# Sums of forms and of weights in place of the blocks they are made of, two places ahead of their splits; a first stage with two pieces fewer; the second weights loaded later

## The chip, the core and the metric

The kernel runs on one core of one Trainium2 chip. The metric is the device time of one execution in microseconds; a figure for a kernel is the median of several runs.

The core's engines work side by side, each through its own queue in order: TensorE (PE, with its weight loads shown apart as PEld), VectorE (DVE), ScalarE (ACT), GpSimd (POOL) and SyncE (SP). Here POOL and SP only issue transfers (DMA): SP loads, POOL stores.

## The reference

```python
def reference(A_x, A_dft_seq_re, A_dft_seq_im, A_dft_hid_re, A_dft_hid_im, B_x, B_w1, B_w3, B_w2, gate_w):
    x = A_x                                              # (1, 2048, 512)
    g = _sigmoid((x * gate_w).sum(-1, keepdims=True))
    a = x @ A_dft_hid_re.T                               # 512 -> 512, real part
    b = x @ A_dft_hid_im.T                               # imaginary part
    fnet = A_dft_seq_re @ a - A_dft_seq_im @ b           # 2048 x 2048 times 2048 x 512, twice
    gate, up = x @ B_w1, x @ B_w3                        # 512 -> 1376
    glu = (_silu(gate) * up) @ B_w2                      # 1376 -> 512
    return g * fnet + (1 - g) * glu
```

(The einsums are written here as products; all in fp32.)

## The kernel before

**Products in three matmuls.** Every fp32 operand is split in two tiles: `hi`, rounded by a copy on ACT (line 71), and `lo`, what is left, by a subtraction on DVE (line 74). A product is then hi·hi + hi·lo + lo·hi: three matmuls (line 81, `mm3`).

**Seven products in place of eight.** Each large product is cut into 2 x 2 blocks and done by a Strassen-Winograd scheme: seven products P1 to P7 of sums of blocks. Sums of the moving operand are called F1 to F4; those of the stationary one ("forms") are, for blocks a11, a12, a21, a22:

- P1: a11, P2: a12, P4: a22 (the blocks themselves)
- P5: a22 - a21
- P6: a11 subtracted from minus P5's sum, -(a22 - a21) - a11
- P7: a11 - a21
- P3: -a12 minus P6's sum

Sums with two minus signs go through `minus_sum` (line 77), one DVE instruction.

**Stages.** (1) The first stage, from the start to some 82 us: 14 steps of `sums_of` / `taken` / `forms_of` for x times the hidden DFT matrices; results go to DRAM as `ab`. (2) The items, to some 289 us: the 1376 columns of w1 and w3 in 11 chunks, `item(c)` for each; the gated products go to DRAM as `hsp`. In odd items and ahead of the first, `second` does an additional product in six parts: PE accumulates into `Yi`, ACT and DVE add what is there to `s` (lines 386 to 398), and PE goes on in the same bank when they have read it. (3) The blocks, to the end: `step` for w2 (m = 0) and for the two sequence DFT matrices (m = 1, 2), whose stationary forms were made in stages 1 and 2.

**Weights of a chunk.** `load_w(c)` loads `ws` (four blocks of 256 columns) on SP's queue, two items ahead. `prep_wa(c)` splits the first two blocks (three for the last chunk) into `wa`. `prep_wb(c)` first calls `sum_wb(c)`, which makes four sums in a fresh tile `wu` (lines 265 to 268), and then splits `wu` into `wb`. `prod` uses them by their place: 0 for F1, 1 for F2, 2 for F3, 3 for B22.

**Pieces of forms.** `forms(m, q, ks, keep)` returns a list of functions, one for the load of two tiles `r` (SP's queue) and one for each product in `ks`: split it into a tile `f` and store that to `fsp` on POOL's queue (with `keep`, the split stays in SBUF for the blocks). `ahead` puts the sum of the next product behind the split of the one before; the sum of the first product stands with the load. Sums P5, P6, P3 and P7 are written to halves of fresh tiles `m`. `inner_forms` does the same for a further product, with tiles `rl`, `ml`, `fl`. The list `later` holds 65 such pieces in order: three sets for m = 0, w2's last rows, three for m = 2, two for m = 1, the inner set. `work(2)` takes two of them at each of the steps 7 to 12 of the first stage (12 in all), and in each item the hooks h0 to h3 take one and h4 takes two. What needs other times is in `tasks`: a table from a step of the first stage to loads and preparations.

**Buffers and order.** Loaded blocks, sums, form tiles, results and some splits share one pool `f4` of 19 buffers (`raw` takes one). A tile takes the buffer of an older tile, and its first writer waits until the older tile's last users are done, a store from it among them. A planner puts the instructions of each engine in order before the kernel runs, by the order of the program and by its own estimate of when each could start; what goes through `pinned`, `keep_in_program_order` or `fetch` keeps the order of the program.

Of the kernel before, what the change touches and what calls it, by code (L numbers as in the profile page):

```python
# [28 lines left out]
def fnet_swiglu_gate_kernel(  # L29
# [17 lines left out]
    nc = tc.nc  # L47
# [11 lines left out]
    def raw(name, n=1024):  # L59
        return f4.tile([P, n], F32, tag="f4", name=name)  # L60

    def half(ap, n=2):
        return ap.rearrange("p (a n) -> p a n", a=n)
# [12 lines left out]
    def minus_sum(o, a, b):  # L76
        nc.vector.scalar_tensor_tensor(o, a, -1.0, b, op0=ALU.mult, op1=ALU.subtract)  # L77
# [181 lines left out]
        WA[c] = half(h, n // 256), half(l, n // 256)  # L259

    def sum_wb(c):
        w = half(WS[c], 4)
        u = raw(f"wu{c}")
        v = half(u, 4)
        nc.vector.tensor_sub(v[:, 0], w[:, 1], w[:, 3])
        minus_sum(v[:, 1], v[:, 0], w[:, 0])
        nc.vector.tensor_sub(v[:, 2], w[:, 0], w[:, 3])
        minus_sum(v[:, 3], v[:, 1], w[:, 2])
        WB[c] = u

    def prep_wb(c):
        if c not in WB:
# [64 lines left out]
    def prod(ps, w, k, xk, start, chain=True):  # L337
        for g in range(G):
            xh, xl = XF[g, xk]
            for q in range(2):  # L340
                sl = slice(q * P, (q + 1) * P)
                mm3(ps[:, g], w[0][:, k, sl], w[1][:, k, sl], xh[:, q], xl[:, q],
                    start and q == 0, q == 1, chain)
# [73 lines left out]
    def item(c, hooks):  # L417
        x, wa, wb = X[c], WA[c], WB[c]

        def part(n):  # L420
            if c % 2 and c + 2 < NC:
                second((c + 1) // 2, n)

        z = pair(3, f"Z{c}")
        u2, u4, g1 = raw(f"u2_{c}"), raw(f"u4_{c}"), None
        prod(x, wb, 1, "F2", False)
        pinned(nc.scalar.activation(u2, flat(x), AF.Copy))
        prod(z, wb, 2, "F3", True)
        pinned(nc.scalar.activation(u4, flat(z), AF.Copy))
        part(0)  # L430
        hooks[0]()
        if c + 1 < NC:
            first1(c + 1)
        if c + 2 == NC:
            begun(c + 1)
        part(1)
        hooks[1]()
        prod(x, wb, 0, "F1", False)
        nc.vector.tensor_add(u4, u4, flat(x))  # L439
        hooks[2]()  # L440
        part(2)
        prod(z, wa, 1, "F4", False)
        nc.vector.tensor_add(u2, u2, flat(z))
        nc.vector.tensor_mul(u2, u2, S1[c])
        store_h(c, 0, u2)
        part(3)
        hooks[3]()
        if c + 2 == NC:
            first2(c + 1)
        hooks[4]()  # L450
        prod(x, wb, 3, "B22", False)
        if c == NC - 1:
            put_score(1, flat(x), -1.0)
        g1 = raw(f"g1_{c}")
        nc.scalar.activation(g1, flat(x), AF.Silu, scale=-1.0)
        if c == NC - 1:
            nc.vector.tensor_mul(u4, u4, g1)
        else:
            nc.vector.scalar_tensor_tensor(u4, u4, -1.0, g1, op0=ALU.mult, op1=ALU.mult)
        store_h(c, 1, u4)  # L460
        part(4)
        part(5)
# [11 lines left out]
    NQS = {0: (NP + 1) // 2, 1: NQ, 2: NQ}  # L474
    A = {}

    def forms(m, q, ks, keep):

        n = width(m, q)
        st = {}  # L480

        def load():
            for h, src in enumerate(rows_of(m, q)):
                st[h] = raw(f"r{m}{q}{h}")
                nc.sync.dma_start(st[h][:, : 2 * n], src[:, : 2 * n])
            st["a11"], st["a21"] = (st[0][:, v * n : (v + 1) * n] for v in range(2))
            st["a12"], st["a22"] = (st[1][:, v * n : (v + 1) * n] for v in range(2))

        def total(k):
            if k in ("P5", "P3") or k == "P7" and "m" not in st:  # L490
                st["m"] = raw(f"m{m}{q}{k}")
            if k == "P5":
                src = st["m"][:, :n]
                nc.vector.tensor_sub(src, st["a22"], st["a21"])
                st["s5"] = src
            elif k == "P6":
                src = st["m"][:, n : 2 * n]
                minus_sum(src, st["s5"], st["a11"])
                st["s6"] = src
            elif k == "P3":  # L500
                src = st["m"][:, :n]
                minus_sum(src, st["a12"], st["s6"])
            elif k == "P7":
                src = st["m"][:, n : 2 * n]
                nc.vector.tensor_sub(src, st["a11"], st["a21"])
            else:
                src = st[{"P1": "a11", "P2": "a12", "P4": "a22"}[k]]
            st[k] = src

        def parts(k):  # L510
            src = st[k]
            pool, tag = (op, "op") if keep else (f4, "f4")
            t = pool.tile([P, 2, n], F32R, tag=tag, name=f"f{m}{k}{q}")
            split(t[:, 0], t[:, 1], src)
            if keep:
                A[m, k, q] = t
            else:
                nc.gpsimd.dma_start(fsp[m, PRODS.index(k), q, :, : 2 * n], flat(t.bitcast(F32)))  # L518

        return ahead(load, total, parts, ks)  # L520

    def ahead(load, total, parts, ks):

        def one(i):
            if i < 0:
                load()
            else:
                parts(ks[i])
            if i + 1 < len(ks):
                total(ks[i + 1])  # L530

        return [lambda i=i: one(i) for i in range(-1, len(ks))]

    def inner_forms():

        st = {}

        def cols(t, v):
            return t.rearrange("p (c h e) -> p c h e", c=4, h=2)[:, :, v]

        def quads(ap):
            return ap.rearrange("p (c e) -> p c e", c=4)

        def load():
            for h in range(2):
                st[h] = raw(f"rl{h}")
                for q in range(2):
                    nc.sync.dma_start(
                        st[h][:, q * 512 : (q + 1) * 512], ab[1, 1, 2 * h + q, :, 0].rearrange("p i e -> p (i e)"))

        def total(k):
            a11, a21, a12, a22 = cols(st[0], 0), cols(st[0], 1), cols(st[1], 0), cols(st[1], 1)
            if k in ("P5", "P3"):
                st["m"] = raw(f"ml{k}")
            lo, hi = quads(st["m"][:, :512]) if "m" in st else None, quads(st["m"][:, 512:]) if "m" in st else None
            if k == "P5":
                src = st["s5"] = lo
                nc.vector.tensor_sub(src, a22, a21)
            elif k == "P6":
                src = st["s6"] = hi  # L560
                minus_sum(src, st["s5"], a11)
            elif k == "P3":
                src = lo
                minus_sum(src, a12, st["s6"])
            elif k == "P7":
                src = hi
                nc.vector.tensor_sub(src, a11, a21)
            else:
                src = {"P1": a11, "P2": a12, "P4": a22}[k]
            st[k] = src  # L570

        def parts(k):
            src = st[k]
            t = f4.tile([P, 2, 512], F32R, tag="f4", name=f"fl{k}")
            split(quads(t[:, 0]), quads(t[:, 1]), src)
            nc.gpsimd.dma_start(lsp[PRODS.index(k)], flat(t.bitcast(F32)))

        return ahead(load, total, parts, ("P1", "P5", "P6", "P3", "P7", "P2", "P4"))

    def load_inner(k):  # L580
        t = A["L", k] = op.tile([P, 2, 4, P], F32R, tag="op", name=f"al{k}")
# [21 lines left out]
    todo = list(INNER)  # L603
# [349 lines left out]
    forms_of(2)  # L953
    later = []
    for q in range(NQS[0]):
        later += forms(0, q, PRODS, False)
    early = len(later)
    later += prep_w2l()
    for q in range(3):
        later += forms(2, q, [k for k in PRODS if k != "P2"], False)  # L960
    for q in range(2):
        later += forms(1, q, ("P1", "P5", "P6", "P3"), False)
    later += inner_forms()
# [1 line left out]
    def work(count):  # L965
        for _ in range(count):
            if later:
# [1 line left out]

    tasks = {2: lambda: load_x(1, "B11"), 3: lambda: load_x(1, "B12"),  # L970
             5: lambda: load_x(1, "B22"), 6: lambda: load_x(1, "B21"),
             7: lambda: load_w(0), 8: lambda: (load_bt(1), load_bt(0), load_w(1)), 9: lambda: (load_wp(0), sum_wb(0), sum_bt()),
             10: lambda: (prep_wa(0), prep_wb(0), sum_wp(0)), 11: lambda: (prep_bt("T3"), prep_bt("T4")),
             12: lambda: (prep_wp(0), prep_bt("T1"))}
    sums_of(0, (0,), True)
    sums_of(1, (0,), True)
    for n in range(len(DSEQ)):
        sums_of(n, (1,) if n < 2 else (0, 1))
        taken(n)
        forms_of(n + 3)  # L980
        tasks.get(n, lambda: None)()
        if 7 <= n < 13:
            work(2)
    first1(0)
    for n in (0, 3, 1, 4, 2, 5):
# [76 lines left out]
    todo += [lambda k=k, q=q: load_a(1, k, q) for k, _ in CHAIN[:4] for q in range(2)]  # L1062
    for i, f in enumerate(todo):
        TASKS.setdefault(AT[0, "P6", 0] + 2 * i if i < 4 else AT[1, "P1", 0] + 2 * i - 6, []).append(f)
    todo = forms(2, 3, [k for k in PRODS if k != "P2"], True)
    todo[:2] = [lambda fs=todo[:2]: [f() for f in fs]]
    todo += [lambda k=k, q=q: load_a(2, k, q) for k in LORDER for q in range(3)]
    for i, f in enumerate(todo):
# [74 lines left out]
```

## Time and profile before

| | us |
|---|---|
| median of 3 runs (701.94 to 702.03) | 701.95 |
| the profiled execution's own time | 703.77 |
| its span in the trace | 701.7 |

Busy shares, in tenths, in 40 slices of the span (17.5 us each):

```profile
PE   9999999999999999999999999999999999999997
PEld 7888888888888788888888888888888888888886
DVE  6999767697878976769998897679785976999985
ACT  6746356365555454474463474445534444544530
PEclk9999999999999999999999999999999999999999
DMA  8387955677887889678459969830989978898923
```

A digit 9 is 90% or more; PEclk is the granted TensorE clock, DMA the mean busy share of the core's 16 DMA engines. In lines of a timeline the columns are start, duration (us), engine, line, operation, `out<-in`, shape, and in brackets the engine's idle time ahead of it and what ended that. A form like `B<-cc` names tiles or DRAM tensors without their numbers.

### The profile page before, as it was taken

The numbers are of one execution on the slowest core, as the hardware profiler recorded it, in microseconds if no ns is written. First come the engines' busy times: TensorE is split into PE (matmuls) and PEld (weight loads), VectorE is DVE, ScalarE is ACT, GpSimd is POOL, SyncE is SP. The second block draws the span as 40 slices with busy tenths as digits, with TensorE's granted clock in tenths as the row PEclk, the third lists the DMA queues.
The fourth block names the chain that finished last, engine by engine and source line by source line (L and its number), as shares of the span: only waits on it lengthen the run. The fifth ranks groups of instructions, "written<-read, shape, count | busy, mean of one in ns | idle before, by whom it ended". The sixth has DMA issues, their size and how long they took to land.

```text
span 701.7 us, 8585 instructions
## 1 busy us (share of the span) xinstructions
PE 695.5 (99%) x3061; PEld 574.1 (82%) x3061; DVE 575.8 (82%) x646; ACT 356.3 (51%) x417; POOL 85.5 (12%) x136
## 2 busy tenths in 40 slices
PE   9999999999999999999999999999999999999997
PEld 7888888888888788888888888888888888888886
DVE  6999767697878976769998897679785976999985
ACT  6746356365555454474463474445534444544530
POOL 0012302131222220000000001000000020110110
PEclk9999999999999999999999999999999999999999
DMA  8387955677887889678459969830989978898923
GB/s 301 138 289 293 344 196 207 226 259 295 293 291 273 303 278 373 233 273 327 161 219 376 356 213 228 286 122 31 339 294 373 341 131 290 210 353 237 218 34 88
DMA packets 54602, 177.00 MB, mean 252 GB/s; under 512 B 5852, under 2 KB 6620, under 8 KB 54560
## 3 DMA queue, kind: packets, MB, share of 16 engines
q1 hardware_dynamic: 35312, 109.98, 44.9%
q0 software_dynamic: 19104, 66.34, 29.2%
q8 instruction: 24, 0.39, 0.2%
q14 instruction: 18, 0.15, 0.1%
q10 hardware_dynamic: 144, 0.13, 0.1%
HBM read 117.96 MB, written 58.47 MB: 251 GB/s over the span
## 4 chain that ended last, share of the span: by engine, by line
PE 91%; issue 5%; POOL 1%; DVE 1%; DMA 1%; DVEq 0%; POOLq 0%
PE P L81 55%; PE X L81 12%; PE dP L81 10%; PE Z L81 6%; PE Lx L81 3%; PE Yi L81 2%; DMA fsp<-f1P 1%; PE Y L81 1%; PE dP L205 1%; POOL fsp L518 1%; PE last L81 1%; PE wps L936 1%; POOL hsp L415 0%; DVE wu L77 0%; DVE s L353 0%
## 5 line engine op out<-in xcount | busy, mean ns | idle before, releaser
L71 ACT ACTIVATE zh<-B 128x1024 fp32r<-128x1024 f32 (+1 forms) x142 | 145.9, 1031 | 169.7 <-PE P L81 136.9
L74 DVE TENSOR_TENSOR zl<-B,zh 128x1024 fp32r<-128x1024 f32 (+1 forms) x142 | 167.1, 1183 | 45.9 <-ACT zh L71 39.0
L81 PE MATMUL P<-zh,f1P 128*128 128x512 f32 x320 | 99.9, 389 | 0.0
L81 PE MATMUL P<-zh,a2P 128*128 128x512 f32 x280 | 88.9, 389 | 0.0
L81 PE MATMUL P<-zh,a0P 128*128 128x512 f32 x280 | 87.6, 389 | 0.0
L677 DVE TENSOR_TENSOR B<-B,B 128x1024 f32<-128x1024 f32 (+1 forms) x70 | 83.6, 1204 | 1.2 <-DMA B<-cc 0.7
L81 PEld LDWEIGHTS P<-zh,f1P 128*128 128x128 f32 x320 | 60.1, 188 | 12.4
L81 PE MATMUL P<-zl,f1P 128*128 128x512 f32 x160 | 62.3, 389 | 0.0
L81 PEld LDWEIGHTS P<-zh,a2P 128*128 128x128 f32 x280 | 52.6, 188 | 10.9
L81 PEld LDWEIGHTS P<-zh,a0P 128*128 128x128 f32 x280 | 52.6, 188 | 10.9
L81 PE MATMUL P<-zl,a0P 128*128 128x512 f32 x140 | 54.5, 389 | 0.0
L81 PE MATMUL P<-zl,a2P 128*128 128x512 f32 x140 | 54.5, 389 | 0.0
L81 PE MATMUL P<-zh,a1P 128*128 128x512 f32 x128 | 40.7, 389 | 0.0
L81 PEld LDWEIGHTS P<-zl,f1P 128*128 128x128 f32 x160 | 30.0, 188 | 6.3
L81 PEld LDWEIGHTS P<-zl,a0P 128*128 128x128 f32 x140 | 26.3, 188 | 5.5
L81 PEld LDWEIGHTS P<-zl,a2P 128*128 128x128 f32 x140 | 26.3, 188 | 5.5
L81 PE MATMUL P<-zh,f2P 128*128 128x512 f32 x88 | 28.9, 389 | 0.0
L81 PEld LDWEIGHTS P<-zh,a1P 128*128 128x128 f32 x128 | 24.0, 188 | 5.0
L81 PE MATMUL P<-zl,a1P 128*128 128x512 f32 x64 | 24.9, 389 | 0.0
L71 ACT ACTIVATE zh<-LB 128x1024 fp32r<-128x1024 f32 x14 | 14.9, 1062 | 19.4 <-PE P L81 18.2
L439 DVE TENSOR_TENSOR u<-u,X 128x1024 f32<-128x1024 f32 x11 | 13.4, 1218 | 10.6 <-PE X L81 10.3
L74 DVE TENSOR_TENSOR zl<-LB,zh 128x1024 fp32r<-128x1024 f32 x14 | 17.1, 1219 | 4.4 <-ACT zh L71 4.4
(1139 smaller groups left out, 1479.8 us busy)
## 6 DMA issues: line engine op xcount, KB each, us to landing
B<-cc SPq DMA_DIRECT2D x56, 512.0 KB, 6.8
r<-ab SPq DMA_DIRECT2D x24, 512.0 KB, 6.0
hsp<-u POOLq DMA_DIRECT2D x18, 512.0 KB, 4.8
fsp<-f2P POOLq DMA_DIRECT2D x18, 512.0 KB, 4.2
a2P<-fsp SPq DMA_DIRECT2D x18, 512.0 KB, 7.3
B<-hsp SPq DMA_DIRECT2D x16, 512.0 KB, 5.1
fsp<-f0P POOLq DMA_DIRECT2D x14, 512.0 KB, 4.2
a0P<-fsp SPq DMA_DIRECT2D x14, 512.0 KB, 7.6
```

The source lines that it names most:

```text
L71: i = nc.scalar.activation(hi, src, AF.Copy)
L74: nc.vector.tensor_sub(lo, src, hi.bitcast(F32))
L81: nc.tensor.matmul(ps, u, v, start=first and n == 0, stop=last and n == 2, skip_group_check=chain)
L205: tc.keep_in_program_order(nc.tensor.matmul(ps[j][:, i], u[:, 0, sl], v[:, 0], start=start, stop=False, skip_group_check=True))
L439: nc.vector.tensor_add(u4, u4, flat(x))
L518: nc.gpsimd.dma_start(fsp[m, PRODS.index(k), q, :, : 2 * n], flat(t.bitcast(F32)))
L677: nc.vector.tensor_add(t, t, RAW[b, o, q])
L936: nc.tensor.matmul(wps[:, 0, :256], ones[:, :P], ones, start=True, stop=True)
```

## The change

- `sum_wb` writes its four sums over the blocks of `ws` itself: place 1 gets F1's, 3 gets F3's, 0 gets F2's and 2 gets B22's, and `item` uses them so. No tile `wu` is taken.
- `sum_a`, new, writes the sums of forms over blocks: P5 over a22, P7 over a21, P6 over a11, P3 over a12. `forms` and `inner_forms` call it; no tiles `m` and `ml` are taken.
- The order of the products of a set, where a block must be split before it is overwritten, becomes P4, P1, P2, P5, P7, P6, P3 (`IN_PLACE`), for m = 0, m = 2 (without P2) and the inner set. The first sets of m = 1 keep P1, P5, P6, P3 and the later ones P7, P2, P4.
- `ahead` puts a sum two places ahead of its split in place of one: those of the first two products stand with the load.
- `work(2)` is called at the steps 7 to 11 of the first stage (10 pieces).
- `load_w(1)` goes from step 8 to step 11, `sum_wb(0)` from step 9 to `prep_wb(0)` in step 10.

```diff
     def sum_wb(c):
         w = half(WS[c], 4)
-        u = raw(f"wu{c}")
-        v = half(u, 4)
-        nc.vector.tensor_sub(v[:, 0], w[:, 1], w[:, 3])
-        minus_sum(v[:, 1], v[:, 0], w[:, 0])
-        nc.vector.tensor_sub(v[:, 2], w[:, 0], w[:, 3])
-        minus_sum(v[:, 3], v[:, 1], w[:, 2])
-        WB[c] = u
+        nc.vector.tensor_sub(w[:, 1], w[:, 1], w[:, 3])
+        nc.vector.tensor_sub(w[:, 3], w[:, 0], w[:, 3])
+        minus_sum(w[:, 0], w[:, 1], w[:, 0])
+        minus_sum(w[:, 2], w[:, 0], w[:, 2])
+        WB[c] = WS[c]
...
-        prod(x, wb, 1, "F2", False)
+        prod(x, wb, 0, "F2", False)
...
-        prod(z, wb, 2, "F3", True)
+        prod(z, wb, 3, "F3", True)
...
-        prod(x, wb, 0, "F1", False)
+        prod(x, wb, 1, "F1", False)
...
-        prod(x, wb, 3, "B22", False)
+        prod(x, wb, 2, "B22", False)
...
+    IN_PLACE = ("P4", "P1", "P2", "P5", "P7", "P6", "P3")
+
+    def sum_a(st, k):
+        if k == "P5":
+            nc.vector.tensor_sub(st["a22"], st["a22"], st["a21"])
+        elif k == "P7":
+            nc.vector.tensor_sub(st["a21"], st["a11"], st["a21"])
+        elif k == "P6":
+            minus_sum(st["a11"], st["a22"], st["a11"])
+        elif k == "P3":
+            minus_sum(st["a12"], st["a12"], st["a11"])
+        return st[{"P1": "a11", "P2": "a12", "P4": "a22", "P5": "a22", "P7": "a21", "P6": "a11", "P3": "a12"}[k]]
...
         def total(k):
-            if k in ("P5", "P3") or k == "P7" and "m" not in st:
-                st["m"] = raw(f"m{m}{q}{k}")
-            if k == "P5":
-                src = st["m"][:, :n]
-                nc.vector.tensor_sub(src, st["a22"], st["a21"])
-                st["s5"] = src
...
-            st[k] = src
+            st[k] = sum_a(st, k)
...
         def one(i):
             if i < 0:
                 load()
+                total(ks[0])
             else:
                 parts(ks[i])
-            if i + 1 < len(ks):
-                total(ks[i + 1])
+            if i + 2 < len(ks):
+                total(ks[i + 2])
...
-        return ahead(load, total, parts, ("P1", "P5", "P6", "P3", "P7", "P2", "P4"))
+        return ahead(load, total, parts, IN_PLACE)
...
     for q in range(NQS[0]):
-        later += forms(0, q, PRODS, False)
+        later += forms(0, q, IN_PLACE, False)
...
     for q in range(3):
-        later += forms(2, q, [k for k in PRODS if k != "P2"], False)
+        later += forms(2, q, [k for k in IN_PLACE if k != "P2"], False)
...
-             7: lambda: load_w(0), 8: lambda: (load_bt(1), load_bt(0), load_w(1)), 9: lambda: (load_wp(0), sum_wb(0), sum_bt()),
-             10: lambda: (prep_wa(0), prep_wb(0), sum_wp(0)), 11: lambda: (prep_bt("T3"), prep_bt("T4")),
+             7: lambda: load_w(0), 8: lambda: (load_bt(1), load_bt(0)), 9: lambda: (load_wp(0), sum_bt()),
+             10: lambda: (prep_wa(0), prep_wb(0), sum_wp(0)), 11: lambda: (load_w(1), prep_bt("T3"), prep_bt("T4")),
...
-        if 7 <= n < 13:
+        if 7 <= n < 12:
             work(2)
...
-    todo = forms(2, 3, [k for k in PRODS if k != "P2"], True)
+    todo = forms(2, 3, [k for k in IN_PLACE if k != "P2"], True)
```

More of the change, by code (lines that the diff above doesn't have):

```diff
@@ L489, in total @@
         def total(k):
-            if k in ("P5", "P3") or k == "P7" and "m" not in st:
-                st["m"] = raw(f"m{m}{q}{k}")
-            if k == "P5":
-                src = st["m"][:, :n]
-                nc.vector.tensor_sub(src, st["a22"], st["a21"])
-                st["s5"] = src
[L496 to L507, printed above, removed]
-            st[k] = src
+            st[k] = sum_a(st, k)
         def parts(k):
@@ L549, in load @@
                         st[h][:, q * 512 : (q + 1) * 512], ab[1, 1, 2 * h + q, :, 0].rearrange("p i e -> p (i e)"))
+            st["a11"], st["a21"], st["a12"], st["a22"] = (cols(st[h], v) for h in range(2) for v in range(2))
         def total(k):
[L552 to L570, printed above, removed]
+            st[k] = sum_a(st, k)
         def parts(k):
```

## The prediction

> **What bounds the kernel now.** I read the busy times first, then TensorE (PE) by stretches, then the chain that ended last, then PE's own waits and the instruction timeline around the largest of them.
>
> ```profile
> PE 695.5 (99%) x3061; PEld 574.1 (82%) x3061; DVE 575.8 (82%) x646; ACT 356.3 (51%) x417; POOL 85.5 (12%) x136
> ...
> 234.00:697.46 463.46, 463.44 (x2045) 1.00 0.76 248
> 11.00:697.46 686.46, 685.35 (x3021) 1.00 0.75 253
> ...
> 289.44 291.04 PE P L81 x1284
> ```
>
> The two rows in the middle are PE alone by stretches: length, busy time, matmuls, granted clock, DMA share, GB/s. PE is busy throughout at clock 1.00. In an undisturbed stretch of the chain (last row) 1284 matmuls take 291.04 us, so 226.67 ns each. The 3021 matmuls of the row 11.00 to 697.46 would need 3021 x 0.22667 = 684.77 us and take 686.46: 1.69 us is all that PE loses after its first 24 matmuls. The change adds and removes no matmul. The first 24, and the few us behind 697.46, it doesn't touch. So no version of this change can gain much over 1.7 us, 0.24%. Where the 1.69 us lies:
>
> ```profile
> 231.23 0.39 PE L81 MATMUL X<-x1F1h,wb7l 128*128 128x512 f32 x1
> 232.71 0.50 PE L81 MATMUL Yi<-x1B21h,wp4zo 128*128 128x512 f32 x1 [1.09 <-DVE s L393]
> 233.05 0.40 PE L81 MATMUL Yi<-x1B21l,wp4zo 128*128 128x512 f32 x1
> ...
> 86.75 0.39 PE L81 MATMUL Z<-x0F3h,wb0l 128*128 128x512 f32 x1
> 87.02 0.51 PE L81 MATMUL Yi<-bth,wp0zo 128*128 128x512 f32 x1
> 87.36 0.40 PE L81 MATMUL Yi<-btl,wp0zo 128*128 128x512 f32 x1
> ...
> 90.14 0.46 PE L81 MATMUL Yi<-x1B21h,wp0zo 128*128 128x512 f32 x1
> 90.44 0.39 PE L81 MATMUL Yi<-x1B21l,wp0zo 128*128 128x512 f32 x1
> ```
>
> From 231.23 to 233.05 two matmuls start in 1.82 us in place of 0.453: **1.37 us** lost. Around 86.75 to 91.4 the starts are late by 0.04, 0.11 and 0.07 us (0.27, 0.34, 0.30 less 0.227) and by some 0.01 at seven others: **0.29 us**. Together 1.66 of the 1.69. Who made PE late at 231?
>
> ```profile
> 223.94 1.22 DVE L459 SCALAR_TENSOR_TENSOR u<-u,g 128x1024 f32<-128x1024 f32 x1
> 229.42 0.43 DVE L265 TENSOR_TENSOR wu<-ws 128x256 f32<-128x256 f32 x1 [4.26 <-DMA fsp<-f1P]
> ...
> 231.98 0.68 DVE L393 TENSOR_TENSOR s<-s,Yi 128x512 f32<-128x512 f32 x1
> ...
> 229.16 0.60 ACT L392 ACTIVATE s<-Yi 128x512 f32<-128x512 f32 x1 [2.18 <-PE Yi L81]
> ```
>
> PE waits for line 393 on VectorE (DVE), whose input from line 392 was there at 229.76. DVE was late because of 4.26 us at line 265: the first sum of chunk 8's weights writes a fresh buffer `wu`, and that buffer's last user, a store of a form (`fsp<-f1P`), hadn't landed. Behind the waiting sum stood another sum, two halves of splits (line 74), two more sums, then line 393. [...]
>
> **The change part by part.**
>
> *Weights summed in place (11 chunks).* `wu` is gone: the four sums write `ws`, whose load and whose other reader, the split `wa`, are issued an item earlier or more. The number of sums is the same. In place and into a fresh tile they cost the same:
>
> ```profile
> L77 DVE SCALAR_TENSOR_TENSOR wu<-wu,ws x22: 415/419/423, 61.8 to 271.6; 128x256 f32<-128x256 f32 x22
> ...
> L265 DVE TENSOR_TENSOR wu<-ws x11: 417/421/427, 61.2 to 268.9; 128x256 f32<-128x256 f32 x11
> ```
>
> (ns, least, median and most; the first group writes `wu` into itself, the second afresh.) So busy time changes by 0. The wait of 4.26 us has nothing left to wait for. Taking it away lets line 393 run when line 392 is done, 229.76, behind at most one such sum in progress (0.43): it ends by 229.76 + 0.43 + 0.68 = 230.87, and PE wants it at 231.46 (231.23 + 0.227). Term: **-1.37 us**. Bounds: 0 if another wait stands there, -1.37 at best.
>
> *Forms summed in place.* The tiles `m` go, two for each of the 3 + 4 + 4 + 1 sets (three for the four sets of m = 1, whose second half took one more): 28 allocations, with `wu` 39 of the 19-buffer pool. Four sums stay four sums. In the inner forms the splits now read strided blocks; a split of such a block (`rl`) and one of a plain sum (`ml`) take 0.69 us both:
>
> ```profile
> 238.39 0.69 DVE L74 TENSOR_TENSOR flP<-rl,flP 128x512 fp32r<-128x512 f32 x1
> ...
> 242.58 0.69 DVE L74 TENSOR_TENSOR flP<-mlP,flP 128x512 fp32r<-128x512 f32 x1
> ```
>
> Price 0. In the order P4, P1, P2, P5, P7, P6, P3 each sum overwrites a block only behind the split that last read it, on the same DVE; no new wait.
>
> *Sums two places ahead.* Where P4, P1, P2 lead, the first sum still comes behind the first split, so nothing of the load is met earlier. Only the sets of m = 1 that keep P1, P5, P6, P3 change: P5's sum now stands with the load itself. Were it placed there on DVE, it would wait for a transfer:
>
> ```profile
> DMA to landing us min/median/max: 2.6/5.7/9.4
> ...
> 193.87 1.29 SPq L485 DMA_DIRECT2D r<-ab  x2
> ...
> 204.01 0.69 DVE L494 TENSOR_TENSOR m10P<-r,r 128x512 f32<-128x512 f32 x1
> 208.80 0.69 DVE L74 TENSOR_TENSOR f1P<-r,f1P 128x512 fp32r<-128x512 f32 x1 [3.77 <-ACT f1P L71]
> ```
>
> The first line is the time to landing of these loads (`r`). The planner already puts this sum (204.01) 8.9 us behind the second load's issue and ahead of the first split. So I take 0; the other bound is a DVE wait of 5.7 to 9.4 us. (That is for two of the sets; the other two come behind 289 us, where each split runs three steps of at least 12 matmuls, 8.2 us, ahead of its use.)
>
> *Two pieces fewer in the first stage.* Ten pieces in place of twelve: of the second set only the load and P4's split stay. Two splits (0.63 us on ScalarE, 0.69 on DVE), three sums of 0.69 and two store issues on POOL (busy 12% of the span) go to later; every later piece, with its loads on SP's queue and stores on POOL's, comes two places later. There were 11 items x 6 = 66 places for 53 pieces, now for 55: the last falls in item 9 in place of item 8. PE has no gap from 234 to 697 that this could close. At 86 to 91, where DVE and ScalarE are late by tenths for line 393, a little less work stands before them: I take half of 0.29, **-0.15 us** (bounds 0 and -0.29).
>
> *Second weights later* (step 11 for step 8). On SP they move behind the plain weights `wp` and ahead of the second set's loads.
>
> ```profile
> 71.11 0.91 SPq L485 DMA_DIRECT2D r<-w  x2
> 84.28 0.33 SPq L249 DMA_DIRECT2D ws<-w  x1
> ...
> DMA to landing us min/median/max: 3.4/4.5/8.1
> ...
> 87.79 0.63 ACT L71 ACTIVATE wa<-ws 128x512 fp32r<-128x512 f32 x1
> ```
>
> The third line is the landing of the weights `ws`. At 71.11 two buffers came free for loads; now `ws1` takes the first of them at the latest and lands by 71.11 + 8.1 = 79.2, 8.6 us ahead of its first reader at 87.79. Cost 0. The two loads behind it slip by one issue, 0.33 us; POOL's stores are not passed.
>
> **Sum.** The profiled execution took 703.77 us, 2.1 over its span of 701.7 and 1.82 over the runs' median of 701.95. 703.77 - 1.37 - 0.15 = 702.25 for it; the same 1.52 off the median gives 700.43, say **700.5**.
>
> **The rivals.**
>
> *The wait moves (A).* DVE is freed of fresh buffers, but form tiles written by ScalarE and loads issued by SP still take them, and their old users are the same stores. For it: DVE also waited 3.77 us at 208.80 for a split that ScalarE did late. Against it: that cost PE nothing, and 39 allocations fewer leave the same 19 buffers more time. It includes the case that the wait at 231 was not the buffer but the work itself. Half to all of the gain is lost: 701.2 to 702.0; I name 701.4.
>
> *DVE sits on a load (B), slower.* Place: P5's sum in the sets of m = 1 in items 6 and 7. It decides from a DVE wait of about 3.8 us: waits up to 3.77 were free, 4.26 cost 1.37, so PE loses the wait less 2.9. A wait of the median 5.7 costs 2.8, the longest 9.4 costs 6.5. From 700.43: 703.2 for one at the median, 706.0 for two; I name **704.3**, nearer the first, since the second set's load has an item in between. Against it stand the 8.9 us above. [...]
>
> *`ws1` comes late (C), slower.* If it gets no buffer before 84.28, where the next weights got theirs, it lands at 92.4 at worst, and ScalarE's `wa`, pinned in order, holds up line 392 behind it by 4.6 us, which PE needs at once (it waits for line 393 at 90.14 already): 700.43 + 4.6 = 705.0. Decides from a landing after 87.8. Against: 8.6 us of slack.
>
> **How the numbers follow.** Forecast 0.55, A 0.18, B 0.20, C 0.07. A measurement of this kernel can tell about 0.2%, 1.4 us, from no change: under 700.55 is faster, over 703.35 slower. The forecast's own range, 700.25 (all 1.69 gone) to 701.0, straddles the first bound; I give 0.37 of its 0.55 to faster and 0.18 to same. A is same; B and C are slower but for 0.01. Faster 0.37, same 0.37, slower 0.26. Range 700.2 to 704.5: it leaves out the longer half of B and of C, 0.14, and a few hundredths below.
>
> **What would show it.** Right: no `wu` rows, no DVE wait at line 265 for `fsp`, PE's own waits empty, 11 to 697 shorter by 1.4 to 1.7. Small term: starts at 86 to 91 within 0.23 us. Planner: P5's sum at least 6 us behind its load. `ws1`: `wa` at about 87.8 without a wait for a DMA. Wrong: any PE gap over 0.5 us after 11 us; its releaser names the rival, DVE behind a load B, ScalarE behind `ws` C, another buffer's store A.

## The result and the profile after

| | before | after |
|---|---|---|
| median of 14 runs each, us | 702.98 (701.94 to 704.73) | 701.17 (700.92 to 701.85) |
| ratio of the times | | 0.9975 [0.9966, 0.9983] |
| profiled execution, us | 703.77 | 701.09 |
| its span, us | 701.7 | 699.3 |

The kernel is faster by 0.25%, 1.76 us by the ratio (1.2 to 2.4). The three runs of before that stood ahead of the prediction, 701.94 to 702.03, are the three fastest of its fourteen.

The page of the changed kernel, its busy times, and PE alone by stretches (length, busy time, matmuls, granted clock, DMA share, GB/s):

```profile
PE 694.6 (99%) x3061; PEld 573.4 (82%) x3061; DVE 577.3 (83%) x646; ACT 356.5 (51%) x417; POOL 85.5 (12%) x136
```

```profile
11.00:695.50 684.50, 684.45 (x3018) 1.00 0.75 254
```

PE is busy in all but 0.05 of 684.50 us; before, 1.11 of 686.46 us were idle. DVE's 646 instructions take 1.5 us more than before, out of 577. Around 231, the same instructions of VectorE as were shown of before:

```profile
222.29 1.22 DVE L459 SCALAR_TENSOR_TENSOR u<-u,g 128x1024 f32<-128x1024 f32 x1
223.42 0.42 DVE L265 TENSOR_TENSOR ws<-ws 128x256 f32<-128x256 f32 x1
...
229.03 0.69 DVE L393 TENSOR_TENSOR s<-s,Yi 128x512 f32<-128x512 f32 x1 [0.82 <-ACT s L392]
```

Line 265 now runs right behind line 459, with no wait for a store; line 393 waits only for its input from line 392. That is what the change was expected to do here, and PE doesn't stop.

Where the span's 2.4 us come from. The last matmul starts at 697.05 before and at 695.13 after, 1.92 us earlier:

- **-1.37**: the gap at 231 is gone.
- **-0.80**: the first 24 matmuls. Before, the first four ran slower. Two rows of each trace, before and then after, show it (x2 is two matmuls; the two groups start 0.99 us apart before, 0.53 after):

```profile
4.45 1.19 PE L205 MATMUL dP<-dB21h,x0B21h 128*128 128x512 f32 x2
5.44 0.96 PE L205 MATMUL dP<-dB21h,x0B21l 128*128 128x512 f32 x2
```

```profile
4.46 0.70 PE L205 MATMUL dP<-dB21h,x0B21h 128*128 128x512 f32 x2
4.99 0.63 PE L205 MATMUL dP<-dB21h,x0B21l 128*128 128x512 f32 x2
```

  The change touches nothing there. It differs from one execution to the next: PE's first matmul of line 81 starts at 10.82 in this trace of before, at 10.48 in a second one of the same kernel (experiment 11) and at 10.02 after; and below, a kernel with all the gain shows the slow first rows again (4.46 and 5.45). So these 0.8 us belong to the executions that were profiled, not to the change.
- **-0.07**: the late starts at 86 to 91 (below).
- **+0.32**: a new small gap at 32:

```profile
31.78 0.61 PE L81 MATMUL dP<-dB22h,x0F4h 128*128 128x512 f32 x2
32.45 0.50 PE L81 MATMUL dP<-dv7h,x0F1h 128*128 128x512 f32 x1
32.78 0.39 PE L81 MATMUL dP<-dv7l,x0F1h 128*128 128x512 f32 x1
```

Two starts take 0.67 and the next 0.33 us, where 0.227 each would make 0.68: 0.32 too much. PE came here 0.8 us earlier, and the work of ScalarE (line 225) that it waited for did not (31.39 against 31.11), so part of what the first matmuls gained went again. The gap is in two of the experiments whose first matmuls were quick (0.30 in 10, 0.11 in 6) and not in two others (2 and 8); it isn't settled whether it belongs to the change or to the execution.

The other 0.45 us lie behind the last matmul: from its start to the span's end 4.65 us before, 4.17 after. This end isn't the mark of a gain: it is 4.58 in the second trace of before (experiment 11), but 4.18 to 4.35 in the other experiments, those that gained nothing among them, and only in 5 it is longer (4.90). And what the measured time has over the span differs as well, in every run:

| run's time less its span, us | runs | median | least, most |
|---|---|---|---|
| before, the runs that stood beside the experiments | 102 | 2.12 | 2.05, 2.20 |
| after | 14 | 1.79 | 1.73, 1.85 |
| before with only the weights in place (below) | 11 | 1.79 | 1.72, 1.82 |

So without the first matmuls the account is 1.37 + 0.07 = 1.44 us on PE's path (1.12 if the gap at 32 counts), 0.45 behind the last matmul and 0.33 outside the span: 2.22 (or 1.90), against 1.76 (1.2 to 2.4) by the ratio. The median spans of those runs, 700.9 for before and 699.35 for after, are 1.55 apart, against 1.89 (or 1.57). Two profiles whose first matmuls took about as long bear it out: before once more (experiment 11) and the change with one load moved back, which does nothing (experiment 9). PE's first matmul of line 81 starts at 10.48 and 10.40 there, its last at 696.62 and 695.21: 1.33 us between. The six other versions with every chunk's weights in place have 1.74 to 1.79 outside the span in the median (1.77 in experiment 7, which gains nothing), the parts of the change with a fresh `wu` 1.87 to 2.01, a `wu` in a buffer of its own 1.77. So it goes with the program; why its end is shorter isn't known.

By an estimate, not every execution of before can have the whole gap at 231. Its shortest span is 699.7 (a run of 701.83). With the earliest start of line 81 (10.02) and the shortest end (4.17) of any trace, 685.5 us would be left for PE's path between, where its two traces, both of executions above the median (703.77 and 703.34), have 686.23 and 686.14. No trace shows an execution of before near 702, so the gap there isn't known.

### The profile page after: what moved, and what is told of

Its sections match the earlier page's. It is cut to its first block, busy times and chain, and to the rows that moved or that the text cites. A ratio compares the mean times of both kernels' runs of the same rounds, so it can differ in the third digit from the quotient of the medians.

```text
span 699.3 us, 8634 instructions
## 1 busy us (share of the span) xinstructions
PE 694.6 (99%) x3061; PEld 573.4 (82%) x3061; DVE 577.3 (83%) x646; ACT 356.5 (51%) x417; POOL 85.5 (12%) x136
## 4 chain that ended last, share of the span: by engine, by line
PE 95%; DVE 2%; DMA 1%; SPq 1%; issue 0%; ACT 0%; DVEq 0%; ACTq 0%
PE P L81 55%; PE X L81 17%; PE Z L81 9%; PE dP L81 7%; PE Lx L81 3%; PE Yi L81 2%; PE Y L81 1%; DMA xB<-xt 1%; PE last L81 1%; SPq L109 0%; DVE dt0P L230 0%; DVE xF L142 0%; DVE xF L145 0%; DVE dv L159 0%; DVE xB L151 0%
## 5 line engine op out<-in xcount | busy, mean ns | idle before, releaser
L74 DVE TENSOR_TENSOR f2P<-r,f2P 128x512 fp32r<-128x512 f32 x24 | 16.1, 682 | 7.1 <-ACT f2P L71 7.1
```

Of the source, the lines that this page charges most:

```text
L74: nc.vector.tensor_sub(lo, src, hi.bitcast(F32))
```

## The experiments

All ratios are to the kernel before, with 95% intervals, on the same chips.

**1. Before, with the weights' sums in place and nothing else** (w_only). The question is which part carries the gain. (Two things go with the sums: their order, and the first chunk's move from step 9 to step 10. Neither was run by itself.)

```diff
-        u = raw(f"wu{c}")
-        v = half(u, 4)
-        nc.vector.tensor_sub(v[:, 0], w[:, 1], w[:, 3])
...
-        WB[c] = u
+        nc.vector.tensor_sub(w[:, 1], w[:, 1], w[:, 3])
+        nc.vector.tensor_sub(w[:, 3], w[:, 0], w[:, 3])
+        minus_sum(w[:, 0], w[:, 1], w[:, 0])
+        minus_sum(w[:, 2], w[:, 0], w[:, 2])
+        WB[c] = WS[c]
...
-        prod(x, wb, 1, "F2", False)
+        prod(x, wb, 0, "F2", False)
...
-             7: lambda: load_w(0), 8: lambda: (load_bt(1), load_bt(0), load_w(1)), 9: lambda: (load_wp(0), sum_wb(0), sum_bt()),
+             7: lambda: load_w(0), 8: lambda: (load_bt(1), load_bt(0), load_w(1)), 9: lambda: (load_wp(0), sum_bt()),
```

> The kernel before with the weights' sums in place alone (forms, the number of pieces and the load of the second weights as before). Theory 1, the loss of before is the fresh buffer of the weights' sums: the PE gap of 1.37 us near 231 is gone, PE has no wait for line 393 there, and the ratio to before is that of the whole change, 0.9975 within 0.0008. Theory 2, the pool of buffers as a whole is too full (11 of the 39 saved allocations are not enough): a gap of 0.5 us or more stays in the items, ratio 0.9985 or more. Theory 3, the first stage's pieces and loads make it: ratio 1.000.

Measured: 0.9978 [0.9969, 0.9986], median 701.38 (700.61 to 701.60). As much as the whole change, as far as the intervals can tell, and no gap of PE after 91 us. Its first matmuls, at 4.46 and 5.45, go at the slower pace that the profile of before has.

**2. The same for chunk 8 alone** (c8_only). The other ten chunks keep their `wu`. If the gain is only the wait at 231, this has it too.

```diff
+    IN_WS = (8,)
...
     def sum_wb(c):
+        if c in IN_WS:
+            return sum_wb_in(c)
...
-        prod(x, wb, 1, "F2", False)
+        prod(x, wb, 0 if c in IN_WS else 1, "F2", False)
```

> The kernel before with the sums in place for chunk 8 alone, the chunk at whose first sum VectorE waited 4.26 us. Theory 1 in its narrow form, one buffer: the gap near 231 is gone and the ratio is as for all chunks, about 0.9975. Theory 1 in its wide form, every fresh buffer of a sum can be late from execution to execution: the gap near 231 is gone from the profile, but the ratio lies between, 0.998 to 0.999, since other chunks' sums are late in other executions. Theory 2: the wait moves to another first writer, a gap of 0.5 us or more at another place, ratio 0.9995 to 1.0005.

Measured: 1.0026 [1.0016, 1.0036], 704.47: slower. The profiled execution, 705.96, is one of the slowest of its twelve. The gap at 231 is gone, and others are there (at 84.67, 224.63, 239.1 and 255.3). Its ScalarE at the second of them, and PE by stretches (lines stand 13 further down in this kernel; L468 is 455):

```profile
224.23 1.06 ACT L71 ACTIVATE wb8h<-ws 128x1024 fp32r<-128x1024 f32 x1 [3.24 <-DVE ws L77]
225.20 1.00 ACT L468 ACTIVATE g<-X 128x1024 f32<-128x1024 f32 x1
```

```profile
224.60:226.30 1.70, 0.47 (x3) 1.00 1.02 388
226.30:230.00 3.70, 3.70 (x16) 1.00 0.43 175
```

ScalarE's queue holds the split of the weights ahead of line 468, which reads PE's bank X and so frees it. The split waits 3.24 us for a sum on VectorE, and PE waits for the bank, 1.2 us of idle time that line 468 ends: 3 matmuls in 1.70 us. In experiment 1 the same two instructions stand in the same order, with a longer wait of the engine, and PE loses nothing; both come 2.55 us earlier:

```profile
221.68 1.06 ACT L71 ACTIVATE wb8h<-ws 128x1024 fp32r<-128x1024 f32 x1 [4.38 <-DVE ws L77]
222.65 1.01 ACT L455 ACTIVATE g<-X 128x1024 f32<-128x1024 f32 x1
```

The idea that the gain is one wait taken away falls. A kernel without that wait can be slower than one with it; what else is needed the next runs ask.

**3. Only the forms in place, two places ahead** (f_only): `sum_a`, `IN_PLACE` and the new `ahead`; weights, pieces and loads as before.

```diff
+    def sum_a(st, k):
...
         def total(k):
-            if k in ("P5", "P3") or k == "P7" and "m" not in st:
-                st["m"] = raw(f"m{m}{q}{k}")
...
+            st[k] = sum_a(st, k)
...
-            if i + 1 < len(ks):
-                total(ks[i + 1])
+            if i + 2 < len(ks):
+                total(ks[i + 2])
```

> The kernel before with the forms' sums in place, their new order and the two places ahead alone (fresh tiles for the weights' sums, 12 pieces, second weights early). Theory 1: VectorE still waits for stores ahead of the weights' sums at line 265, by 3 us or more somewhere, and the ratio is 0.999 to 1.001. Theory 2: 28 allocations fewer are enough, no wait at line 265 over 1 us, ratio about 0.9975.

Measured: 0.9999 [0.9990, 1.0008], 703.06: no change. Its VectorE's wait at line 265 (total us, times, longest):

```profile
DVE wu L265 <- DMA hsp<-u: 2.6, 2, 1.6
```

In the trace of before line 265 waits three times, at 114 (3.21), 189 (1.93) and 229 (4.26), and only the last costs PE. Here it waits at 112 and 187, for other stores and by less than the 3 us expected, and at 225.7 by 0.07. PE's gaps are others: 0.58 at 155.9 for line 393, which stood behind splits, and 0.37 at 237.4 for line 359, which stood behind splits that had waited 2.78 us for their load. So the 28 allocations saved in the forms shorten these waits, don't end them all, and gain nothing in time.

**4. Only the first stage's pieces and the load of the second weights** (s_only).

```diff
-             7: lambda: load_w(0), 8: lambda: (load_bt(1), load_bt(0), load_w(1)), 9: lambda: (load_wp(0), sum_wb(0), sum_bt()),
-             10: lambda: (prep_wa(0), prep_wb(0), sum_wp(0)), 11: lambda: (prep_bt("T3"), prep_bt("T4")),
+             7: lambda: load_w(0), 8: lambda: (load_bt(1), load_bt(0)), 9: lambda: (load_wp(0), sum_wb(0), sum_bt()),
+             10: lambda: (prep_wa(0), prep_wb(0), sum_wp(0)), 11: lambda: (load_w(1), prep_bt("T3"), prep_bt("T4")),
...
-        if 7 <= n < 13:
+        if 7 <= n < 12:
```

> The kernel before with 10 pieces in the first stage and the second weights loaded at step 11, sums as before. Theory 1: the wait at line 265 and the gap stay or move with the pieces, ratio 0.999 to 1.002. Theory 3: gap gone, ratio about 0.9975.

Measured: 1.0026 [1.0016, 1.0036], 704.81: slower. The gap at 231 is gone here too, though `wu` is still fresh, and gaps at 66.0, 224.48, 262 and 275.9 took its place. At 224, the load, VectorE and ScalarE:

```profile
208.99 1.52 SPq L485 DMA_DIRECT2D r<-ab  x2
...
217.02 0.69 DVE L494 TENSOR_TENSOR m10P<-r,r 128x512 f32<-128x512 f32 x1 [1.19 <-DMA r<-ab]
...
224.48 0.63 ACT L71 ACTIVATE f1P<-m10P 128x512 fp32r<-128x512 f32 x1 [2.23 <-DVE m10P L77]
225.02 1.00 ACT L455 ACTIVATE g<-X 128x1024 f32<-128x1024 f32 x1
```

P5's sum (line 494) waits for its load; the sums and splits behind it come late; and the last split shown stands ahead of line 455, for which PE waits 1.21 us. Two pieces fewer at the start shift every later piece by two hooks, and so which piece meets which instruction of an item.

**5. The change with fresh `wu`** (a_wu): the edit of experiment 1 undone in the changed kernel.

```diff
+        u = raw(f"wu{c}")
+        v = half(u, 4)
+        nc.vector.tensor_sub(v[:, 0], w[:, 1], w[:, 3])
...
-        WB[c] = WS[c]
+        WB[c] = u
```

> The changed kernel with the weights' sums back in fresh tiles (the first chunk's sums back at step 9); forms in place, two places ahead, 10 pieces and the late second weights stay. The weights in place alone gave 0.9978, the forms alone 0.9999, the schedule alone 1.0026. If the weights carry the gain and the rest adds: 1.002 to 1.003, with a PE gap of 0.5 us or more at an odd item. If the rest is worth as much once the schedule is changed as well (the parts help each other): 0.998 or less.

Measured: 1.0037 [1.0020, 1.0054], 705.14 (703.87 to 709.30): slower than before, and by 0.6% slower than the change. The parts of experiments 3 and 4 are a loss together when the weights aren't summed in place. Its ScalarE:

```profile
237.87 0.63 ACT L71 ACTIVATE f1P<-r 128x512 fp32r<-128x512 f32 x1 [0.57 <-DVE r L77]
238.47 1.01 ACT L359 ACTIVATE Y<-X 128x1024 f32<-128x1024 f32 x1
```

A split that waits for a sum of its set stands ahead of line 359, and PE stops for that line, 2.10 us. Line 265 has no wait for a store in this trace. What is late here is the set's load, issued at 224.29, where the change has 221.40; the set's first sum, P5's, waits for it, and the other sums and the splits follow:

```profile
234.21 0.69 DVE L482 TENSOR_TENSOR r<-r,r 128x512 f32<-128x512 f32 x1 [0.87 <-DMA r<-ab]
```

**6. Sums one place ahead** (a_one): in the changed kernel.

```diff
                 load()
-                total(ks[0])
...
-            if i + 2 < len(ks):
-                total(ks[i + 2])
+            if i + 1 < len(ks):
+                total(ks[i + 1])
```

> The changed kernel with the forms' sums one place ahead of their splits as before. If the two places ahead are what keeps ScalarE from waiting for a sum (as it did by 1.9 and 2.2 us ahead of line 455 in the run with the schedule alone): ScalarE waits for VectorE's sums of forms again, a PE gap of 0.5 us or more in the items, ratio 0.9985 to 1.000. If the place of the sums doesn't matter: 0.9975 within 0.001.

Measured: 0.9973 [0.9964, 0.9983], 701.43. Not to be told from the change: a place more or less does nothing that these runs can tell.

**7. Twelve pieces in the first stage** (a_12): in the changed kernel.

```diff
-        if 7 <= n < 12:
+        if 7 <= n < 13:
             work(2)
```

> The changed kernel with 12 pieces in the first stage as before. By the prediction's small term the starts at 86 to 91 are later by 0.1 to 0.2 us and the ratio rises by 0.0002, too little to tell: 0.9975 to 0.998. If the two pieces were costly there (a queue of VectorE that reaches into the first item): 0.9985 or more. If they cost where they go, as in the run with the schedule alone: 0.997 or less.

Measured: 1.0000 [0.9989, 1.0010], 703.35 (702.36 to 705.17). The whole gain is gone. The profiled execution is the slowest of its twelve runs. Its ScalarE, and PE by stretches:

```profile
157.09 0.60 ACT L397 ACTIVATE s<-Yi 128x512 f32<-128x512 f32 x1 [2.80 <-PE Yi L81]
...
162.38 1.15 ACT L71 ACTIVATE f2P<-r 128x512 fp32r<-128x512 f32 x2 [4.69 <-DMA r<-ab]
163.44 1.00 ACT L359 ACTIVATE Y<-X 128x1024 f32<-128x1024 f32 x1
```

```profile
162.00:164.50 2.50, 0.50 (x4) 1.00 0.43 147
164.50:166.00 1.50, 1.50 (x7) 1.00 0.88 257
166.00:169.30 3.30, 3.30 (x9) 0.50 0.88 348
```

A split of a form waits 4.69 us for its load, ahead of line 359; PE stands for 2.16 us and then runs 9 matmuls in 3.30 us at half clock. In the changed kernel no split stands between the same two lines, 397 and 359:

```profile
157.00 0.60 ACT L397 ACTIVATE s<-Yi 128x512 f32<-128x512 f32 x1 [1.70 <-PE Yi L81]
158.47 1.01 ACT L359 ACTIVATE Y<-X 128x1024 f32<-128x1024 f32 x1 [0.87 <-DVE s L398]
```

**8. Twelve pieces, and two taken out of item 0** (a_12p): experiment 7, and at hook h4 as below. From item 1 on the pieces then meet the hooks as in the changed kernel.

```diff
                 prep_wa(c + 2)
-            work(2)
+            work(2 if c else 0)
```

> The changed kernel with 12 pieces in the first stage, and two pieces fewer in the first item, so that from the second item on every piece stands where it stands in the changed kernel. In the run with 12 pieces alone two splits of a set just loaded stood in ScalarE's queue ahead of line 359 in item 3, waited 4.7 us for the load and cost PE 2.2 us and a halved clock behind it. Theory 4, what counts is which piece meets which hook of an item: the gap near 162 is gone and the ratio is 0.9975 within 0.001, as for the changed kernel. Rival, two pieces more in the first stage are themselves too much: a gap of 0.5 us or more before 100 us, or 0.9985 or more.

Measured: 0.9967 [0.9955, 0.9979], 700.96 (700.58 to 701.69, 7 runs), not to be told from the change. The same twelve pieces, and no gap. So it isn't their number in the first stage that counts, but which piece meets which hook of an item. ScalarE's lines 397 and 359 follow each other as in the changed kernel, at 156.71 and 158.19.

**9. The second weights loaded at step 8 again** (a_w1), in the changed kernel.

```diff
-8: lambda: (load_bt(1), load_bt(0)),
+8: lambda: (load_bt(1), load_bt(0), load_w(1)),
...
-11: lambda: (load_w(1), prep_bt("T3"), prep_bt("T4")),
+11: lambda: (prep_bt("T3"), prep_bt("T4")),
```

> The changed kernel with the second weights loaded at step 8 as before. Forecast: no difference, 0.9975 within 0.001, since the load has 8 us to spare at either place. Rival: the buffer that it holds for three steps longer makes the second set of forms late, its first split on ScalarE after 82 us, and PE late by 0.5 us or more at 84 to 91: 0.9985 or more.

Measured: 0.9973 [0.9962, 0.9983], 701.24. The moved load does nothing that these runs can tell.

**10. Weights in place with ten pieces and the late load, old forms** (w_s): the edits of experiments 1 and 4 together.

> The kernel before with the weights' sums in place, 10 pieces and the late second weights; forms in tiles of their own and in their old order. Theory 4: as in the run with the schedule alone, three splits that each wait for a sum stand in ScalarE's queue ahead of line 455 in item 6; a PE gap of 0.5 to 1.5 us near 224, ratio 0.999 to 1.002. Rival, the weights in place carry the gain whatever the pieces do: no gap, 0.9975 within 0.001.

Measured: 0.9974 [0.9964, 0.9984], 701.56. The gap of experiment 4 at 224 did not come. The same rows as there:

```profile
203.29 1.58 SPq L485 DMA_DIRECT2D r<-ab  x2
...
214.16 0.68 DVE L494 TENSOR_TENSOR m10P<-r,r 128x512 f32<-128x512 f32 x1
...
221.40 0.63 ACT L71 ACTIVATE f1P<-m10P 128x512 fp32r<-128x512 f32 x1 [2.19 <-DVE m10P L77]
221.94 1.01 ACT L455 ACTIVATE g<-X 128x1024 f32<-128x1024 f32 x1
```

The order is the same, splits of forms ahead of line 455; but the loads were issued 5.70 us earlier (203.29 against 208.99), P5's sum met no wait, and line 455 ran 3.08 us earlier. What held the loads up is in SyncE's waits at this place, of experiment 4 and then of 10 (total us, times, longest):

```profile
SPq L485 <- DMA hsp<-u: 5.7, 1, 5.7
...
SPq L485 <- DMA fsp<-f2P: 0.8, 1, 0.8
```

Both are stores of other tiles; the wait of experiment 4, which ends at 208.99, is as long as the difference. Eleven tiles fewer from the pool of 19, and this load got its buffers 5.70 us sooner: the weights in place have this second effect, beside the wait at line 265.

**11. The kernel before once more** (b_again), with no edit, for a second trace of it.

> The kernel before, unchanged, profiled once more: its runs spread over 3.5 us, those of the changed kernel over 1.0. If the wait of VectorE at line 265 for a store to land is what spreads them, VectorE waits at line 265 again, but by another length or at other chunks, and PE's gap behind it differs from 1.37 us by 0.3 us or more; with no gap at 231 the time is near 700.5 to 701.5.

Measured: one execution, 703.34, span 701.2. Its VectorE's wait, with PE idle for 1.02 us for line 393 behind it:

```profile
DVE wu L265 <- DMA fsp<-f1P: 4.2, 1, 4.2
```

The wait and the gap are in both traces of before, 1.29 us of lost starts here against 1.37, so less of a difference than was expected. Both are of executions above the median, so whether the wait is what sets its runs 2.8 us apart, and those of the change 0.9, stays open.

**12. `wu` with a buffer of its own** (wu_own), in the kernel before.

```diff
-    f4 = ctx.enter_context(tc.tile_pool(name="f4", bufs=19, side="right"))
+    f4 = ctx.enter_context(tc.tile_pool(name="f4", bufs=18, side="right"))
+    wx = ctx.enter_context(tc.tile_pool(name="wx", bufs=1, side="right"))
...
-        u = raw(f"wu{c}")
+        u = wx.tile([P, 1024], F32, tag="wu", name=f"wu{c}")
```

> The kernel before with the weights' sums in a fresh tile still, but in one buffer of their own, and 18 buffers in the common pool in place of 19, so that the memory is the same. Theory 1, what counts is that VectorE's first sum doesn't wait for another tile's store: no wait at line 266 (265 before) for a transfer, no gap near 231, ratio 0.9975 to 0.9985. Theory 2, what counts is room in the common pool, which lets the forms' loads start earlier: the loads of the sets wait as before or longer, gaps at other places of the items, ratio 0.9995 or more.

Measured: 1.0016 [1.0003, 1.0028], 704.32. No gap at 231; new ones at 84.9, 251.9 (1.26) and 612.5 (1.13), the last far behind the items. To keep `wu` from waiting is not enough when a buffer is taken from all the others. This run changes two things at once, the tile's place and the pool's size; a version with 19 and one more wasn't run.

## Why the prediction was right, step by step

- **The gap at 231, -1.37.** Right in mechanism and size for the traces: the wait at line 265 is gone, so is PE's. For the median run of before the gap's size isn't known.
- **Sums in place cost nothing on VectorE.** Right: 575.8 to 577.3 us of busy time, none of it in PE's way. But "right" is weaker than it looks for the forms: alone they bring nothing (experiment 3), and their half of the change isn't needed (experiments 1 and 10).
- **Two places ahead, 0.** Right (experiment 6). Rival B's wait did not occur in the change: P5's sum is 9.6 us behind the end of its loads' issues (8.9 before, counted the same way) and has no wait. With fresh `wu` it did, by 0.87 us (experiment 5).

```profile
221.40 1.22 SPq L499 DMA_DIRECT2D r<-ab  x2
...
232.26 0.69 DVE L482 TENSOR_TENSOR r<-r,r 128x512 f32<-128x512 f32 x1
```

- **Second weights later, 0.** Right (experiment 9), and `wa` ran at 87.33, without a wait for a transfer; rival C falls.

- **Two pieces fewer, -0.15.** Mis-sized: 0.29 us of late starts became 0.22, so -0.07. The three late starts of before, by 0.04, 0.11 and 0.07, are still there, by 0.03, 0.11 and 0.05 (0.26, 0.34 and 0.28 less 0.227):

```profile
86.30 0.39 PE L81 MATMUL Z<-x0F3h,wb0l 128*128 128x512 f32 x1
86.56 0.50 PE L81 MATMUL Yi<-bth,wp0zo 128*128 128x512 f32 x1
86.90 0.40 PE L81 MATMUL Yi<-btl,wp0zo 128*128 128x512 f32 x1
...
89.86 0.44 PE L81 MATMUL Yi<-x1B21h,wp0zo 128*128 128x512 f32 x1
90.14 0.40 PE L81 MATMUL Yi<-x1B21l,wp0zo 128*128 128x512 f32 x1
```

  The larger fault of this step is its sentence that two splits, three sums and two stores "go to later", at no cost. They could have cost 1.8 us (experiment 4, 0.26%) or the whole gain (experiment 7, the same pieces moved back). That the shift was harmless here is a matter of which split came ahead of which line; the step didn't look at that order, so that its price came out near nothing was luck.
- **"The first 24, and the few us behind 697.46, it doesn't touch."** The second half failed. PE's path gave 1.12 to 1.44 us of the forecast's 1.52; another 0.78 came from behind the last matmul, 0.45 inside the span and 0.33 outside. The argument for "no version of this change can gain much over 1.7 us" falls with it: it bounds PE's path alone. The measured 1.76 (1.2 to 2.4) isn't clearly over that bound.
- **"The same 1.52 off the median"** was taken off three runs at the fast end of before, which by the estimate above can't have the whole gap that the sum takes away. Against all fourteen the change is worth 1.8 us in medians, while the time itself came to 701.17, 0.7 above the forecast: the start was 1.03 too low and the gain 0.29 too small. That the two errors partly cancel is luck.
- **Rival A, the wait moves.** It didn't in the whole change. In parts of the change it did: in experiments 2, 3, 4, 5, 7 and 12 another tile, load or split held PE up, by up to 2.2 us a gap.
- **The clock.** The prediction had no row for what a longer gap does to it. These runs have: behind 2.00 us idle out of 2.50 (experiment 7) the clock went to 0.50 for over 3 us, behind 1.23 out of 1.70 (experiment 2) it stayed 1.00, as behind the 1.09 us idle of before at 231.

What carries the gain, then, is the weights summed in place, in two ways. The first sum no longer waits for the store of another tile: shown at line 265. And with eleven tiles fewer from the pool the loads of forms are issued earlier: shown by the rows of experiments 4 and 10 at one place, 5.70 us there, and the late load of experiment 5 fits it. That it is the cause in all of the parts that were slower is argued from the same pattern, not shown in each.

No run beats the change clearly: experiment 8's 0.9967 [0.9955, 0.9979] and the change's 0.9975 [0.9966, 0.9983] overlap.

## What to carry to other kernels

Ask of a fresh tile whose store its buffer waits for, and what stands behind its first writer in that engine's queue; sums written over their own blocks took that wait away (4.26 us at line 265) and gave the pool room (loads issued 5.70 us earlier at one place); here, where the blocks had no reader left, that cost nothing. When pieces of work are handed out by hooks, look not at their number but at which split or sum then stands ahead of an instruction that frees a PE bank: moved by two places, the same pieces cost nothing (0.9967, experiment 8) or the whole gain (1.0000, experiment 7). And account for the time behind the last matmul and outside the span in both kernels: over a third of the difference between these two profiles, the first matmuls apart, was there, and versions without the gain had it too.

## What the runs showed of the hardware

A gap of PE cost more than its length in the two traces where PE was idle for 1.93 and 2.00 us, and not where it was idle for 1.23 us or less; two cases don't fix where it begins. In experiment 7 PE was idle for 2.00 us up to 164.5; for 1.5 us more the clock was full, and then it was half. PE's first and last start of that stretch, at 165.99 and 169.63, are nine matmuls apart: 3.64 us for nine, where 2.04 would do: 1.6 us lost behind the gap, three quarters of the gap's own 2.16. Experiment 5 shows the same: the gap (1.93 idle), 1.2 us mostly at full clock, then half clock.

```profile
237.00:239.60 2.60, 0.67 (x4) 1.00 1.05 425
239.60:240.80 1.20, 1.20 (x5) 0.90 1.05 430
240.80:243.90 3.10, 3.10 (x8) 0.50 1.00 363
```

The first matmuls of line 205 ran at a slower pace in some executions than in others, up to four of them and 0.8 us in all: two traces of the same kernel (before, and experiment 11) differ by 0.34 us there.
